# Four row tiles per VectorE operation in the FFN steps, filter products handed out by a time quota, and the columns of a small table made first

## The chip, the cores and the metric

The kernel runs on one core of a Trainium2 chip. The metric is the device time of one execution in microseconds (us). Each ratio comes with a 95% interval, and a difference counts as faster or slower only from 2% on.

Engines: PE is TensorE (PEld its weight loads), DVE is VectorE, ACT is ScalarE, POOL is GpSimd, SP issues most of the transfers. A row tile is 128 of the 2048 rows. "A step" below is one (g, m): a slice g of 256 FFN columns (18 of them) with a quarter m = 0..3 of the 16 row tiles, 72 steps in all. PSUM is the memory that the matmuls write into: each piece of work takes one of its buffers, and has to wait until the result before it has been copied out. SBUF holds all other tiles.

## The reference, cut to what matters

The function is a gated mix of two branches on one input, and the kernel computes its output and the gradients of seven inputs.

```python
g = _sigmoid((x * gate_w).sum(-1, keepdims=True))
a = irfft2(rfft2(x) * (w_r + 1j * w_i))            # filter branch, 2048 x 576
b = (gelu(x @ w_gate) * (x @ w_up)) @ w_down       # FFN branch, F = 4608
return g * a + (1 - g) * b                         # and the VJP of all this
```

In the kernel the Fourier transforms are matmuls against tables that it makes itself (cosines and sines of D columns, of 16-point columns "B", and so on). They are woven into the 72 FFN steps, so that PE always has one of three kinds of work: FFN matmuls (`xy`, `z`), weight-gradient pieces (`wps`), and Fourier matmuls (`fx`, `pf`).

## The kernel before: the parts concerned

The elementwise work of a step, once for each two row tiles: four operations before the two sigmoids, eight after them.

```python
def H_ew1(xy, q):
    xb, s, hu = (ewt(n) for n in ("xb", "s", "hu"))
    nc.scalar.copy(xb[:], xy[:, :, 0:FG]); nc.scalar.copy(hu[:], xy[:, :, FG:2 * FG])
    V.tensor_scalar(s[:], q[:], A_GELU, 1.0, ...)         # q = gate half squared, made by ACT
    V.tensor_tensor(s[:], xb[:], s[:], op=ALU.mult)
    ... # two more on q
def H_ew2(g, tp, tiles, da):
    nc.scalar.activation(om[:], s[:], ACT.Sigmoid, scale=-2.0 * C_GELU)
    nc.scalar.activation(s[:], s[:], ACT.Sigmoid, scale=2.0 * C_GELU)
    ... # eight DVE operations make A, dHg, dHu
```

The order of work in a step (cut). `sig0` and `sig1` are the two halves' sigmoids; after each of them DVE gets up to three filter products, whatever they cost. `hs` are the weight-gradient pieces of the step.

```python
def side_work():
    for _ in range(3):
        if side:
            side.pop(0)()
...
jobs = [(0, sig0)] * bool(carry) + carry + [(1.7, second)] + [(0, sig0)] * (not carry) + hs
```

The weight-gradient pieces of a slice: four down-projection pieces d, four pieces w, a small rest. Each needs one of the two PSUM buffers of the pool `pw` and gives it back when ACT (now and then DVE) has copied the piece out (`dwd`, `dw`). The last line spreads them over the four steps m = 0..3 of the next slice.

```python
pw = ps1.enter_context(tc.tile_pool(name="pw", bufs=2, space=PSUM, **kw))
...
return [[d[0]], [d[1], w[0]], [d[2], d[3], tl_], [w[1], w[2]], w[3]]
```

## Time and profile before

| | before |
|---|---|
| time, median of 4 runs beside the change | 1488.5 us (1486.2 to 1490.6) |
| span of the profiled run | 1480.0 us |
| PE busy | 1406.3 us (95%) |
| DVE busy | 880.3 us (59%) |
| ACT busy | 724.3 us (49%) |
| granted TensorE clock, mean | 0.983 |

PE bounds the kernel, so time can be won only from PE's waits and from its slow clock. The windows of the kernel before show where those lie: in 240 to 640 us, the steps that carry both filter work and weight gradients, PE is busy 373 of 400 us and the clock is 0.96; from 640 us on it is nearly full.

```profile
core 0: us, PE busy (x) PEld busy (x) DVE busy (x) ACT busy (x) POOL busy (x), PEclk, DMA share, GB/s
...
240.00:640.00 400.00, 372.84 (x2854) 256.05 (x2852) 325.59 (x879) 281.29 (x551) 36.16 (x57) 0.96 0.48 125
640.00:1030.00 390.00, 388.69 (x3274) 280.81 (x3272) 290.44 (x793) 265.25 (x527) 39.21 (x61) 1.00 0.55 142
```

### The profile page before, as it was taken

How to read it: one execution, taken by the hardware profiler on the slowest of the kernel's cores; microseconds unless marked ns; L12 is line 12 of the kernel's file. 1: busy time of each engine (PE TensorE's matmuls, PEld its weight loads, DVE VectorE, ACT ScalarE, POOL GpSimd, SP SyncE). 2: the span in 40 equal slices, each digit the busy share in tenths (PEclk: the TensorE clock that was granted, in tenths of full speed). 3: DMA queues.
4: the chain of work that ended last, by engine and by line, in shares of the span. 5: the costliest groups of instructions: out<-in, count | busy, mean ns of one | idle time of the engine just before them, and what ended most of it. 6: DMA issues, size and time to landing. Idle time of an engine off the chain costs nothing.

```text
span 1480.0 us, 29784 instructions
## 1 busy us (share of the span) xinstructions
PE 1406.3 (95%) x11412; PEld 1028.8 (70%) x11412; DVE 880.3 (59%) x2359; ACT 724.3 (49%) x1424; POOL 126.0 (9%) x230
## 2 busy tenths in 40 slices
PE   6789899898999999999999999999999999999998
PEld 4446576575675675677777777677877777777776
DVE  6598668978877878867777778775000561212110
ACT  5587568577676677667767766664000000000000
POOL 2101010010010010010010011000000110000000
PEclk9999999999999999999999999999999999999999
DMA  5154344554455454354545545656999997777773
GB/s 191 52 142 129 98 117 124 134 136 126 125 137 123 126 137 127 101 142 129 129 132 149 149 134 150 171 142 140 267 201 202 200 220 163 163 161 163 157 155 74
DMA packets 519990, 215.21 MB, mean 145 GB/s; under 512 B 316296, under 2 KB 514056, under 8 KB 519848
## 3 DMA queue, kind: packets, MB, share of 16 engines
q1 hardware_dynamic: 510216, 192.80, 55.9%
q0 software_dynamic: 7824, 19.49, 4.4%
q8 instruction: 89, 1.46, 0.4%
q10 hardware_dynamic: 1808, 1.02, 0.2%
q14 instruction: 53, 0.43, 0.1%
HBM read 40.90 MB, written 93.84 MB: 91 GB/s over the span
## 4 chain that ended last, share of the span: by engine, by line
PE 77%; DVE 14%; ACT 5%; issue 2%; DMA 1%; POOL 0%; SPq 0%; DVEq 0%; ACTq 0%; POOLq 0%
PE acc L1084 28%; PE xy L385 14%; PE wps L496 12%; PE wps L479 7%; PE z L373 6%; PE wps L509 2%; PE xy L380 2%; PE z L376 1%; DVE sn L703 1%; DVE sm L703 1%; DVE om L438 1%; DVE A L436 1%; ACT da L398 1%; DVE s L412 1%; PE fx L547 1%
## 5 line engine op out<-in xcount | busy, mean ns | idle before, releaser
L1084 PEld LDWEIGHTS <-pin 128*128 128x128 bf16 x3456 | 338.0, 98 | 86.2 <-DMA pin<-scr 1.2
L385 PE MATMUL xy<-wgu,xT 128*128 128x512 bf16 x1152 | 282.7, 391 | 0.0
L496 PEld LDWEIGHTS <-xn 128*128 128x128 bf16 x2304 | 224.7, 98 | 31.1 <-issue 0.2
L385 PEld LDWEIGHTS <-xT 128*128 128x128 bf16 x1152 | 109.2, 100 | 145.5 <-issue 43.3
L398 ACT ACTIVATE da<-z,omg 128x256 bf16<-128x256 f32 x288 | 113.3, 475 | 112.0 <-PE z L376 110.3
L1101 ACT COPY bo<-acc 128x288 f32<-128x288 f32 x32 | 12.8, 399 | 309.1 <-PE acc L1084 309.1
L479 PE MATMUL wps<-dB,A 128*128 128x288 bf16 x1152 | 155.2, 289 | 0.0
L373 PE MATMUL z<-wdT,dOT 128*128 128x256 bf16 x1152 | 139.4, 275 | 13.4 <-ACT Y L554 7.2
L1084 PE MATMUL acc<-wgT,pin 128*128 128x288 bf16 x1152 | 143.6, 286 | 0.0
L1084 PE MATMUL acc<-wuT,pin 128*128 128x288 bf16 x1152 | 143.6, 286 | 0.0
L1084 PE MATMUL acc<-wd_all,pin 128*128 128x288 bf16 x1152 | 142.8, 286 | 0.9 <-DMA pin<-scr 0.9
L479 PEld LDWEIGHTS <-A 128*128 128x128 bf16 x1152 | 113.5, 99 | 37.6 <-issue 2.5
L373 PEld LDWEIGHTS <-dOT 128*128 128x128 bf16 x1152 | 111.8, 98 | 32.1 <-issue 13.6
L496 PE MATMUL wps<-dHg,xn 128*128 128x256 bf16 x1152 | 133.0, 273 | 0.0
L496 PE MATMUL wps<-dHu,xn 128*128 128x256 bf16 x1152 | 132.0, 272 | 0.0
L404 ACT ACTIVATE q<-xy 128x512 bf16<-128x512 f32 x144 | 86.8, 603 | 63.9 <-PE xy L385 62.9
L428 ACT ACTIVATE om<-s 128x512 bf16<-128x512 bf16 x144 | 92.6, 643 | 51.7 <-DVE s L412 51.7
L1161 DVE SCALAR_TENSOR_TENSOR f32t<-gwf,dlog,b16t 128x576 f32<-128x576 f32 x16 | 13.1, 818 | 173.9 <-DMA b16t<-dxa_scr 173.9
L411 DVE TENSOR_SCALAR s<-q 128x512 bf16<-128x512 bf16 x144 | 41.9, 291 | 89.5 <-ACT q L404 89.2
L429 ACT ACTIVATE s<-s 128x512 bf16<-128x512 bf16 x144 | 90.7, 630 | 4.6
L412 DVE TENSOR_TENSOR s<-xb,s 128x512 bf16<-128x512 bf16 x144 | 61.2, 425 | 52.5 <-ACT xb L409 46.0
L502 POOL DMA_DIRECT2D out_dram<-dw x67 | 48.8, 729 | 458.9 <-ACT dw L457 334.0
(196 smaller groups left out, 1762.9 us busy)
## 6 DMA issues: line engine op xcount, KB each, us to landing
scr<-A SPq DMA_DIRECT2D x144, 128.0 KB, 2.1
scr<-dHg SPq DMA_DIRECT2D x144, 128.0 KB, 2.1
scr<-dHu SPq DMA_DIRECT2D x144, 128.0 KB, 2.2
out_dram<-dw POOLq DMA_DIRECT2D x67, 128.0 KB, 2.4
wd_all<-in_B_w_down_dram SPq DMA_DIRECT2D x3, 1728.0 KB, 14.3
out_dram<-dwd POOLq DMA_DIRECT2D x34, 144.0 KB, 2.2
scr_p<-Vt SPq DMA_DIRECT2D x32, 145.0 KB, 2.9
wgu<-in_B_w_gate_dram SPq DMA_DIRECT2D x18, 256.0 KB, 3.3
```

Of the source, the lines that this page charges most:

```text
L373: nc.tensor.matmul(zo(t), lhsT=dOT[:, ci, t, :], rhs=wdT[:, ci, :], start=(t % 4 < 2 and ci == 0), stop=False)
L385: nc.tensor.matmul(xy[k][:, t % 2, :], lhsT=xT[:, ci, t, :], rhs=wgu[:, ci, :], start=False, stop=(ci == 3))
L398: nc.scalar.activation(da[:, tt, :], z[:, tt, k, :], ACT.Copy, scale=omg32[:, t:t + 1])
L404: nc.scalar.activation(q[:], xy[:, :, 0:FG], ACT.Square)
L411: V.tensor_scalar(s[:], q[:], A_GELU, 1.0, op0=ALU.mult, op1=ALU.add)
L412: V.tensor_tensor(s[:], xb[:], s[:], op=ALU.mult)
L428: nc.scalar.activation(om[:], s[:], ACT.Sigmoid, scale=-2.0 * C_GELU)
L429: nc.scalar.activation(s[:], s[:], ACT.Sigmoid, scale=2.0 * C_GELU)
L479: nc.tensor.matmul(wps[:, :288], lhsT=tl(0, t)[:, fch * P:(fch + 1) * P], rhs=dB[:, t, h * 288:(h + 1) * 288], start=(t == 0), stop=(t == ...
L496: nc.tensor.matmul(wps[:, cc, :], lhsT=xn[:, t, (c0 + cc) * P:(c0 + cc + 1) * P], rhs=tl(k, t), start=(t == 0), stop=(t == T - 1))
L502: wst[0].dma_start(ov[:, c0:c0 + TPB, fsl], dw[:])
L1084: nc.tensor.matmul(acc[:, :288], lhsT=src[:, r, :], rhs=w_of(r)[:, h * 288:(h + 1) * 288], start=(first and r == 0), stop=(last and r == F ...
```

## The change

Its intent is to make DVE lighter and its work more even: (1) the FFN elementwise work in operations on four row tiles, with a formula of 2 + 9 operations in place of 4 + 8; (2) filter products in 14 units of known length, handed out by a quota of 1.4 us at two places a step; (3) the copies of a tail table moved from DVE to ACT; (4) the columns of table B made at the very start and the rest of B inside the loop. Larger tiles need SBUF, so fewer are kept, and the weight-gradient pieces were put in another order so that the `A` tiles come free sooner. Cut to its core:

```diff
-    keepA = ... bufs=13      # two row tiles each
+    keepA = ... bufs=6       # four row tiles each
 def H_ew1 / H_ew2:           # now on [P, 4, FG] tiles, q, s and om with one buffer
-        V.tensor_tensor(q[:], xb[:], q[:], op=ALU.mult)
 ...
+        V.tensor_tensor(xb[:], xb[:], s[:], op=ALU.mult)
+        V.tensor_tensor(q[:], xb[:], q[:], op=ALU.mult)
         V.tensor_tensor(om[:], om[:], q[:], op=ALU.mult)
-        V.tensor_scalar(om[:], om[:], 1.0, None, op0=ALU.add)
 ...
+        V.tensor_tensor(om[:], om[:], s[:], op=ALU.add)
+        V.tensor_tensor(hu[:], da[:], hu[:], op=ALU.mult)
+        V.tensor_tensor(dHg[:], hu[:], om[:], op=ALU.mult)
 # weight-gradient pieces for m = 0, 1, 2, 3
-        return [[d[0]], [d[1], w[0]], [d[2], d[3], tl_], [w[1], w[2]], w[3]]
+        return [[d[0]], [d[1], d[2], d[3]], [w[0], tl_], [w[1], w[2]], w[3]]
 # quota
-            def side_work():
-                for _ in range(3):
-                    if side:
-                        side.pop(0)()
+            def side_work(us):
+                while side and us > 0:
+                    us -= side[0][0]
+                    side.pop(0)[1]()
 # order in a step: one pair of sigmoids, after the first job behind `second`
-                jobs = [(0, sig0)] * bool(carry) + carry + [(1.7, second)] + [(0, sig0)] * (not carry) + hs
+                jobs = carry + [(1.7, second)] + hs
                 for w, f in jobs:
                     ...
                     f()
+                    if f is not second and state and late:
+                        late.pop()()
 # tail table
-        V.tensor_copy(tb.Oi[:, :, 0:P], tp_[:, :, 0:P])        # and three more
+        nc.scalar.copy(tb.Oi[:, :, 0:P], tp_[:, :, 0:P])
 # head
     build_D(nc, tb, unit, res, 0, 2)
+    columns_B(nc, tb, res)
     build_D(nc, tb, unit, res, 2, 2)
 ...
+        if t == 13:
+            build_B(nc, tb, unit, res)
-    build_B(nc, tb, unit, res)
```

More of the change, by code (lines that the diff above doesn't have):

```diff
@@ L75, in iotas @@
     nc.vector.tensor_scalar(tb.dn[:], tb.dcol[:], 1.0 / D, None, op0=ALU.mult)
-    tb.krow = res.tile([P, 32, 2, 2], F32, name="krow")
+    kk = tb.kk = unit([2, P], F32, name="kk")
+    tb.krow = kk[:, 0, :].rearrange("p (g k c) -> p g k c", k=2, c=2)
     for v in range(2):
@@ L79, in iotas @@
     G.memset(tb.krow[:, 0, 1, :], 32.0)
-    tb.kadd = res.tile([P, 64, 2], F32, name="kadd")
-    G.iota(tb.kadd[:], pattern=[[0, 64], [S // 4, 2]], base=S // 4, channel_multiplier=0, **kw)
+    tb.kadd = kk[:, 1, :].rearrange("p (k c) -> p k c", c=2)
+    G.iota(tb.kadd, pattern=[[0, 64], [S // 4, 2]], base=S // 4, channel_multiplier=0, **kw)
     tb.scol = res.tile([P, T], F32, name="scol")
@@ L145, in build_R @@
     X = unit([n, P], I32, name="XR")
-    krow, kadd = tb.krow[:].rearrange("p g k c -> p (g k c)"), tb.kadd[:].rearrange("p k c -> p (k c)")
+    krow, kadd = tb.kk[:, 0, :], tb.kk[:, 1, :]
     for t in range(n):
@@ L154, in build_R, with columns_B @@
     tb.Rt += [tb.Rpair[:, t0 % 8 + t, :] for t in range(n)]
-def build_B(nc, tb, unit, res):
+def columns_B(nc, tb, res):
     V, G = nc.vector, nc.gpsimd
-    kw = dict(allow_small_or_imprecise_dtypes=True)
     col = res.tile([P, 12], F32, name="bcol")
@@ L188, in build_B @@
     tt(m1, u_, k_, ALU.add)
+    tb.bcols = (k_, nt, a0, a1, b1, m0, m1)
+def build_B(nc, tb, unit, res):
+    V, G = nc.vector, nc.gpsimd
+    kw = dict(allow_small_or_imprecise_dtypes=True)
+    k_, nt, a0, a1, b1, m0, m1 = tb.bcols
     k2 = unit([2, 2, 16, 2], F32, name="k2B")
@@ L242 @@
     o5v = out_5[0:512, :].rearrange("(c p) f -> p c f", p=P)
-    scr = [[dram.tile([TPB, P, FF], BF16, name=f"scr{k}_{tp}") for tp in range(NT)] for k in range(3)]
+    scr = [[dram.tile([4, P, FF], BF16, name=f"scr{k}_{m}") for m in range(T // 4)] for k in range(3)]
     a_scr = dram.tile([S, D], BF16, name="a_scr")
@@ L297 @@
     load_w(0, 0)
-    gwb = res.tile([P, D], BF16, name="gwb")
     ew = wstack.enter_context(tc.tile_pool(name="ew", bufs=2))
-    keepA = wstack.enter_context(tc.tile_pool(name="keepA", bufs=13))
-    keep = wstack.enter_context(tc.tile_pool(name="keep", bufs=16))
+    keepA = wstack.enter_context(tc.tile_pool(name="keepA", bufs=6))
+    keep = wstack.enter_context(tc.tile_pool(name="keep", bufs=8))
     stage = wstack.enter_context(tc.tile_pool(name="stage", bufs=2))
@@ L389, in ewt, with H_act, H_ew1 @@
     def ewt(tag):
-        return ew.tile([P, TPB, FG], BF16, tag=tag, name=tag, bufs=3 if tag in ("da", "xb") else 2)
+        return ew.tile([P, 4, FG], BF16, tag=tag, name=tag, bufs=1 if tag in ("q", "s", "om") else 2)
     def H_da(m, z):
-        das = []
-        for k in range(2):
-            da = ewt("da")
-            for tt in range(TPB):
-                t = 4 * m + 2 * k + tt
-                nc.scalar.activation(da[:, tt, :], z[:, tt, k, :], ACT.Copy, scale=omg32[:, t:t + 1])
-            das.append(da)
-        return das
-    def H_q(xy):
-        q = ewt("q")
-        nc.scalar.activation(q[:], xy[:, :, 0:FG], ACT.Square)
-        return q
-    def H_ew1(xy, q):
-        xb, s, hu = (ewt(n) for n in ("xb", "s", "hu"))
-        nc.scalar.copy(xb[:], xy[:, :, 0:FG])
-        nc.scalar.copy(hu[:], xy[:, :, FG:2 * FG])
+        da = ewt("da")
+        for t in range(4):
+            nc.scalar.activation(da[:, t, :], z[:, t % 2, t // 2, :], ACT.Copy, scale=omg32[:, 4 * m + t:4 * m + t + 1])
+        return da
+    def H_act(k, xy, tiles, part):
+        xb, q, hu = tiles
+        h = slice(2 * k, 2 * k + 2)
+        if part == 0:
+            nc.scalar.activation(q[:, h, :], xy[:, :, 0:FG], ACT.Square)
+        else:
+            nc.scalar.copy(xb[:, h, :], xy[:, :, 0:FG])
+            nc.scalar.copy(hu[:, h, :], xy[:, :, FG:2 * FG])
+    def H_ew1(tiles):
+        xb, q, hu = tiles
+        s = ewt("s")
         V.tensor_scalar(s[:], q[:], A_GELU, 1.0, op0=ALU.mult, op1=ALU.add)
@@ L413, in H_ew1 @@
         V.tensor_scalar(q[:], q[:], 6.0 * A_GELU * C_GELU, 2.0 * C_GELU, op0=ALU.mult, op1=ALU.add)
-        V.tensor_tensor(q[:], xb[:], q[:], op=ALU.mult)
-        return xb, q, s, hu
+        return s
     stores = []
@@ L423, in flush, with H_ew2 @@
             n -= 1
-    def H_ew2(g, tp, tiles, da):
-        xb, q, s, hu = tiles
+    def H_ew2(g, m, tiles, s, da):
+        xb, q, hu = tiles
         om = ewt("om")
@@ L429, in H_ew2 @@
         nc.scalar.activation(s[:], s[:], ACT.Sigmoid, scale=2.0 * C_GELU)
-        A = keepA.tile([P, TPB, FG], BF16, tag="A", name="A")
-        dHg = keep.tile([P, TPB, FG], BF16, tag="dHg", name="dHg")
-        dHu = keep.tile([P, TPB, FG], BF16, tag="dHu", name="dHu")
+        A = keepA.tile([P, 4, FG], BF16, tag="A", name="A")
+        dHg = keep.tile([P, 4, FG], BF16, tag="dHg", name="dHg")
+        dHu = keep.tile([P, 4, FG], BF16, tag="dHu", name="dHu")
+        V.tensor_tensor(xb[:], xb[:], s[:], op=ALU.mult)
+        V.tensor_tensor(q[:], xb[:], q[:], op=ALU.mult)
         V.tensor_tensor(om[:], om[:], q[:], op=ALU.mult)
-        V.tensor_scalar(om[:], om[:], 1.0, None, op0=ALU.add)
-        V.tensor_tensor(xb[:], xb[:], s[:], op=ALU.mult)
         V.tensor_tensor(A[:], xb[:], hu[:], op=ALU.mult)
-        V.tensor_tensor(om[:], om[:], s[:], op=ALU.mult)
-        V.tensor_tensor(om[:], om[:], hu[:], op=ALU.mult)
-        V.tensor_tensor(dHg[:], da[:], om[:], op=ALU.mult)
         V.tensor_tensor(dHu[:], da[:], xb[:], op=ALU.mult)
+        V.tensor_tensor(om[:], om[:], s[:], op=ALU.add)
+        V.tensor_tensor(hu[:], da[:], hu[:], op=ALU.mult)
+        V.tensor_tensor(dHg[:], hu[:], om[:], op=ALU.mult)
         fsl = slice(g * FG, (g + 1) * FG)
@@ L443, in store @@
             for k, tl in enumerate((A, dHg, dHu)):
-                LD.dma_start(scr[k][tp][:, :, fsl].rearrange("t p f -> p t f"), tl[:])
+                LD.dma_start(scr[k][m][:, :, fsl].rearrange("t p f -> p t f"), tl[:])
         stores.append(store)
@@ L463, in tl @@
         def tl(k, t):
-            return kt[t // TPB][k][:, t % TPB, :]
+            return kt[t // 4][k][:, t % 4, :]
         dwd_tiles, wp = {}, {}
@@ L520, in W_units @@
         if g == 0:
-            return [[w[0], tl_], [w[1], d[0]], [d[1], d[2], d[3]], [w[2], w[3]], []]
-        return [[d[0]], [d[1], w[0]], [d[2], d[3], tl_], [w[1], w[2]], w[3]]
+            return [[w[0], tl_], d, [w[1]], [w[2]], w[3]]
+        return [[d[0]], [d[1], d[2], d[3]], [w[0], tl_], [w[1], w[2]], w[3]]
     side = []
@@ L585, in tail_table @@
             nc.tensor.transpose(tp_[0:n, c, 768:768 + 32], tb.Dt[3][0:32, c, P:HF], ident[0:32, 0:32])
-        V.tensor_copy(tb.Oi[:, :, 0:P], tp_[:, :, 0:P])
-        V.tensor_copy(tb.Oi[:, :, P:HF], tp_[:, :, 512:512 + n])
+        nc.scalar.copy(tb.Oi[:, :, 0:P], tp_[:, :, 0:P])
+        nc.scalar.copy(tb.Oi[:, :, P:HF], tp_[:, :, 512:512 + n])
         ot = unit([2, HF], name="ot")
-        V.tensor_copy(ot[0:n, :, 0:P], tp_[0:n, :, 256:256 + P])
-        V.tensor_copy(ot[0:n, :, P:HF], tp_[0:n, :, 768:768 + n])
+        nc.scalar.copy(ot[0:n, :, 0:P], tp_[0:n, :, 256:256 + P])
+        nc.scalar.copy(ot[0:n, :, P:HF], tp_[0:n, :, 768:768 + n])
         for c in range(2):
@@ L693, in comb, with stack @@
                 return f
-            def stack(k1, k2, conj):
+            def stack(k1, k2, conj, j):
                 def f():
-                    m1, m2 = st[p, k1], st.pop((p, k2))
-                    o = unit([2, 2, DF], name="s" + k1)
-                    for j in range(2):
-                        J = slice(64 * j, 64 * j + 64)
-                        for c, op in enumerate(signs(conj)):
-                            V.tensor_tensor(o[64 * c:64 * c + 64, :, j, :], m1[J, :, c, :], m2[J, :, 1 - c, :], op=op)
-                    st[p, k1] = o
+                    m1, m2 = st[p, k1], st[p, k2]
+                    if j == 0:
+                        st[p, "s" + k1] = unit([2, 2, DF], name="s" + k1)
+                    o = st[p, "s" + k1]
+                    J = slice(64 * j, 64 * j + 64)
+                    for c, op in enumerate(signs(conj)):
+                        V.tensor_tensor(o[64 * c:64 * c + 64, :, j, :], m1[J, :, c, :], m2[J, :, 1 - c, :], op=op)
                 return f
@@ L709, in f @@
                 def f():
-                    m = st[p, key][:].rearrange("p t j l -> p (t j) l")
+                    if key == "m1":
+                        halve(st[p, "sm1"])
+                    m = st[p, "s" + key][:].rearrange("p t j l -> p (t j) l")
                     q = unit([4, 2, HF], name="q" + key)
@@ L726, in products @@
             return [
-                lambda: halve(G),
-                mul("m1", X, W[:, 0]), mul("m2", X, W[:, 1]), stack("m1", "m2", False),
-                lambda: (halve(st[p, "m1"]), fold("m1")()),
-                mul("n1", G, W[:, 0]), mul("n2", G, W[:, 1]), lambda: (stack("n1", "n2", True)(), fold("n1")()),
-                mul("o1", G, X[:, :, 0, :]), mul("o2", G, X[:, :, 1, :]), comb("o1", "o2", True),
-                out_dw,
+                (0.9, lambda: (halve(G), mul("m1", X, W[:, 0])())), (0.8, mul("m2", X, W[:, 1])),
+                (0.85, stack("m1", "m2", False, 0)), (0.85, stack("m1", "m2", False, 1)), (1.2, fold("m1")),
+                (0.8, mul("n1", G, W[:, 0])), (0.8, mul("n2", G, W[:, 1])),
+                (0.85, stack("n1", "n2", True, 0)), (0.85, stack("n1", "n2", True, 1)), (1.1, fold("n1")),
+                (0.8, mul("o1", G, X[:, :, 0, :])), (0.8, mul("o2", G, X[:, :, 1, :])), (0.85, comb("o1", "o2", True)),
+                (0.0, out_dw),
             ]
@@ L863 @@
             x2[t - 2]()
+    run_late(tb)
     x2[T - 2]()
-    build_B(nc, tb, unit, res)
-    run_late(tb)
     x2[T - 1]()
@@ L936 @@
             hs = [h for u in pend[m] for h in u] if pend else []
-            def side_work():
-                for _ in range(3):
-                    if side:
-                        side.pop(0)()
+            def side_work(us):
+                while side and us > 0:
+                    us -= side[0][0]
+                    side.pop(0)[1]()
             if g == 0 and m > 0:
@@ L944 @@
             z, xy_full = H_mm(g, m)
+            tiles = [ewt(tag) for tag in ("xb", "q", "hu")]
             xy = xy_full(0)
-            das = H_da(m, z)
-            q = H_q(xy)
+            da = H_da(m, z)
+            H_act(0, xy, tiles, 0)
             flush()
@@ L953 @@
                 fft_next()
-            ta = H_ew1(xy, q)
+            H_act(0, xy, tiles, 1)
             state = []
-            def sig0():
-                H_ew2(g, 2 * m, ta, das[0])
-                side_work()
-                state.append(None)
             def second():
@@ L965, in second, with sigs @@
                     fft_next()
-                state.insert(0, H_ew1(xy, H_q(xy)))
-            def sig1():
-                H_ew2(g, 2 * m + 1, state[0], das[1])
-                side_work()
+                for part in range(2):
+                    H_act(1, xy, tiles, part)
+                state.append(H_ew1(tiles))
+                side_work(1.4)
+            def sigs():
+                H_ew2(g, m, tiles, state[0], da)
+                side_work(1.4)
             if g == 0:
@@ L973 @@
                 fft_next()
-                sig0()
-                sig1()
+                sigs()
             else:
-                jobs = [(0, sig0)] * bool(carry) + carry + [(1.7, second)] + [(0, sig0)] * (not carry) + hs
+                jobs = carry + [(1.7, second)] + hs
                 us = sum(j[0] for j in jobs)
-                at, k, late = 0.0, 1, [sig1]
+                at, k, late = 0.0, 1, [sigs]
                 for w, f in jobs:
@@ L983 @@
                         k += 1
-                        if len(state) == 2 and late:
-                            late.pop()()
                     f()
                     at += w
+                    if f is not second and state and late:
+                        late.pop()()
                 while k <= n:
@@ L990 @@
                     k += 1
-                if late:
-                    sig1()
+                assert not late
             carry = []
@@ L996 @@
                 load_w(g + 1, m)
-            if pr == 3:
-                LD.dma_start(gwb[:], gate_w.partition_broadcast(P))
             if (g, m) in ((0, 3), (1, 0)):
@@ L1020, in pin @@
         tl = p2in.tile([P, FCB, P], BF16, tag="pin", name="pin")
-        LD.dma_start_transpose(tl[:], scr[k][t // TPB][t % TPB][:, f0 * P:(f0 + FCB) * P])
+        LD.dma_start_transpose(tl[:], scr[k][t // 4][t % 4][:, f0 * P:(f0 + FCB) * P])
         return tl
@@ L1068 @@
         gwf = p2res.tile([P, D], F32, name="gwf")
-        V.tensor_copy(gwf[:], gwb[:])
         wT_loads = [(k, r0) for k in range(NB) for r0 in (0, 6)]
@@ L1076, in b16t, with load_gwf @@
             return p2b.tile([P, D], BF16, tag="b16t", name="b16t")
+        def load_gwf():
+            gwb = b16t()
+            LD.dma_start(gwb[:], gate_w.partition_broadcast(P))
+            V.tensor_copy(gwf[:], gwb[:])
         def acc_pair():
@@ L1190 @@
                 load_wuT(*wT_loads.pop(0))
+            if i == 8:
+                load_gwf()
             lead = lead and kind != "u"
```

## The prediction

> **What bounds the kernel now.** I read the page first: over the span of 1480.0 us TensorE (PE) is busy 1406.3 us (95%), VectorE (DVE) 59%, ScalarE (ACT) 49%. So a faster DVE is worth nothing by itself; only PE's idle 73.7 us, and whatever makes its matmuls slow, can be won. The slices show where: DVE and ACT work only up to about 1040 us; the last 30% (matmuls of line 1084) is PE at 100% and the change leaves it alone. Next the table of who waited for whom on PE over the whole span (engine line waited for: total us, times, longest):
>
> ```profile
> PE pf L744 <- ACT da L398: 25.4, 7, 4.7
> PE xy L380 <- ACT g_bf L354: 7.8, 1, 7.8
> PE z L373 <- ACT Y L554: 7.2, 4, 2.1
> ...
> PE z L373 <- DVE ot L590: 4.3, 1, 4.3
> PE pf L564 <- ACT ve L568: 1.9, 1, 1.9
> PE z L373 <- ACT Vt L747: 1.7, 1, 1.7
> ```
>
> Seven stalls, one for each of seven filter passes, make 25.4 us. The timeline around the first one tells what they are:
>
> ```profile
> 284.37 0.43 DVE L412 TENSOR_TENSOR s<-xb,s 128x512 bf16<-128x512 bf16 x1
> ...
> 284.83 0.63 ACT L428 ACTIVATE om<-s 128x512 bf16<-128x512 bf16 x1 [4.77 <-DVE s L412]
> ...
> 286.03 1.55 ACT L398 ACTIVATE da<-z,omg 128x256 bf16<-128x256 f32 x4
> ...
> 287.63 0.64 PE L744 MATMUL pf<-qn,BTtab 128*128 128x290 bf16 x2 [4.75 <-ACT da L398]
> ...
> 288.07 3.62 PE L385 MATMUL xy<-wgu,xT 128*128 128x512 bf16 x8
> ...
> 300.75 1.90 PE L385 MATMUL xy<-wgu,xT 128*128 128x512 bf16 x8
> ```
>
> Read backwards: the filter matmul needs the PSUM buffer that z and the FFT share; `da` empties it, but stands on ACT behind a sigmoid that waited 4.77 us for `s` of a late DVE. On DVE's timeline there is no gap from 254.6 to 288 us: products are issued three at a time after each of the two elementwise parts of a step, some 6 us of them in one step, on top of 9.35 us of FFN work, while a step is 13.9 us of PE. On average DVE is only 81% busy from 240 to 640 us; it is overloaded in bursts.
>
> The last two lines show a second cost: right after a stall eight matmuls took 3.62 us, elsewhere 1.90. In the chain of work the eight after the seven stalls take 3.41, 3.37, 2.96, 3.41, 3.01, 3.19 and 2.86 us against 1.83: 9.4 us more; the down-projection matmuls behind them lose 2.3 more. So the seven stalls cost 25.4 + 11.7 us.
>
> The 7.8 us is the head's end. The small table B is built there last:
>
> ```profile
> 48.75 0.17 DVE L166 CAST bcol<-bbit 128x4 f32<-128x4 int32 x1
> 49.09 0.35 POOL L170 TENSOR_SCALAR bcol<-bcol 128x1 f32<-128x1 f32 x2 [40.23 <-DVE bcol L166]
> ...
> 56.01 0.51 ACT L213 ACTIVATE oB<-XBi,pi 128x256 f32<-128x256 int32 x1 [9.57 <-DVE XBi L206]
> ...
> 58.35 0.61 PE L380 MATMUL xy<-wgu,xT 64*128 64x512 bf16 x2 [7.77 <-ACT g_bf L354]
> ```
>
> The gate's sigmoid stands on ACT behind B's sine, and PE behind the gate's PSUM buffer.
>
> **What the Trainium skill says.** "TensorE: Matmul & The Clock Gate", What's actually happening: after an idle window of about 3.4 us the array runs at half rate, until a busy window has passed. The trace agrees: the 4.75 us stall is followed by matmuls at half rate, and the granted clock of 280 to 320 us is 0.91. The same page, Architectural detail, has ACT and DVE as strict FIFOs; the trace agrees, since `da` ran only after both sigmoids. "VectorE: DVE Perf Modes", The perf-mode tier table: bf16 from SBUF, a tensor_tensor does two elements a cycle, a tensor_scalar four. The trace agrees: 425 ns at 512 elements and 757 ns at 1156 give 0.516 ns an element and some 160 ns fixed, which doubling the tile saves. "ScalarE: Activation LUTs", What ACT_TABLE_LOAD costs: an ACTIVATE is 186 ns + 0.833 ns an element; that makes 613 ns at 512, the trace has 643 and 630.
>
> **The change part by part.**
>
> 1. FFN elementwise. Groups of VectorE before (72 steps, 144 instructions a line):
>
> ```profile
> L412 DVE TENSOR_TENSOR s<-xb,s 128x512 bf16<-128x512 bf16 x144 | 61.2, 425 | 52.5 <-ACT xb L409 46.0
> L411 DVE TENSOR_SCALAR s<-q 128x512 bf16<-128x512 bf16 x144 | 41.9, 291 | 89.5 <-ACT q L404 89.2
> L682 DVE TENSOR_TENSOR o<-Xg,Xx 128x1156 bf16<-128x1156 bf16 x16 | 12.1, 757 | 0.0
> ```
>
> A step now has 18 tensor_tensor and 6 tensor_scalar: the twelve rows sum to 673 us, 9.35 us a step. After: 9 tensor_tensor of 1024 elements, estimated 425 + 512 x 0.516 = 689 ns, and 2 tensor_scalar, estimated 291 + 133 = 424 ns (512 more at four a cycle of 0.96 GHz, that page's clock): 7.05 us. Saved 2.3 us a step, 166 us of DVE in all, nearly all beside PE. The sigmoids go from four of 0.636 to two of about 1.06 us: 0.43 us of ACT a step.
>
> 2. Products by quota. A pass has 6 multiplications of 0.757, 8 stackings of 0.457, 4 folds of 0.462, a combination of 0.92 and small ones of 0.7: 11.7 us. Now each of two places a step issues units until 1.4 us are spent, in fact 1.6 to 1.7. That is 3.3 us a step, so 10.4 us of DVE against 12.5 to 13 of PE (13.9 less the stall's share). In the built program of the change qn is made in the step before the one that uses it, about 10 us ahead. For the sigmoid: the first ACT copies of the second half end about 1.2 us after its matmuls, `s` is done 1.1 later, both sigmoids 2.1 after that, `da` 2.0 later with a copy between: 6.4 us, where PE has 16 down-projection matmuls, z and xy of the next step, 6.5 us, before it wants the buffer in the tightest step. So the stalls should shrink to a few tenths. Gain: 25.4 + 11.7, with the 1.7 us of `Vt`, 38.8; I leave 1.8 for such remains: **37 us**.
>
> 3. tail_table's copies go from DVE (behind two elementwise parts) to ACT ahead of the sigmoids, four copies of about 1.1 us in sum, beside 16 matmuls of 1.96 us. The 4.3 us go, and z after it at half rate (3.60 against 1.91 us, with its small followers 2.2 in all): **6.5 us**. FFT units lie a little differently in that step, which should remove most of the 1.9 us for `ve`: **1.5 us**.
>
> 4. The head. The 7.8 us and 1.6 of slow matmuls after it should go. But the columns are now ahead of the D tables on POOL: nine tiny DVE operations take 1.3 us there, 14 POOL ones 3.5 us (49.1 to 52.6 above), and POOL makes y of tables 2 to 4 only then. Before, the cosine work on DVE ended at 6.7 us and PE's first full run of L547 began at 11.0. After: bits to 8.0, columns to 11.7, y to 13.1, DVE's X and its copies of xT to 15.9, the last table to 17.7. PE starts 6.6 us later. The rest of B in the loop costs 2 to 3 us of DVE and ACT on a path where both alternate with PE. Net 9.4 - 6.6 - 2.5 = **0.3 us**.
>
> 5. The first group (58 to 105 us) has ACT without gaps at 10.3 us a step and PE waiting 1.7 us for `Y`; 0.4 us less of ACT in three steps: **1 us**. The gate weights loaded late, the stores of four tiles and the reordered W units move nothing on PE; both programs have equal counts of PE instructions (22826 rows).
>
> Sum: 37 + 6.5 + 1.5 + 0.3 + 1 = 46 us; 1489.8 - 46 = 1444, and I add 2 for waits that single buffers of q, s and om may bring: **1446 us**.
>
> **The rivals.** (a) The stalls come back as another wait: one H_ew1 for four tiles waits for the second half, so the sigmoids come later and `da` with them. For: ACT is a FIFO and the tightest step has only 0.1 us to spare. Against: DVE has 2 us a step free, so it isn't behind when the copies arrive. Should each pass keep two stalls of 1.5 us (too short for the slow clock), 8 passes keep 24 us: about 1468. (b) The head loses: a start 6.6 us later and a longer B wait, say 5 us in all beyond my net: 1451. (c) The slow clock goes more fully than counted: granted clock 0.983 over 1480 us means 25 us lost, of which I claim 15.5; with g = 0 also free of waits: 1434. (d) Single buffers delay ACT: Square of the next step waits for DVE's third product of this one; in the tightest step both fall at about 6.5 us after the second half's matmuls, so a few tenths, and the buffer of xy is wanted again only half a step later: I expect nothing on PE.
>
> **Range and chances.** The mechanism of part 2 is shown directly and DVE gets lighter by 25%, so faster by over 2% (under 1460) has 0.86; rival (a) in earnest gives within 2%, 0.13; slower 0.01. Range 1433 to 1462.
>
> **What would show it right or wrong.** Right: line `pf <- ACT da` gone or under 3 us; DVE's FFN operations near 690 and 425 ns and its busy time down by some 165 us; granted clock at or above 0.99 between 240 and 640 us; `ot` gone from PE's waits; the first long run of PE's first table matmuls at 17 us instead of 11; `g_bf` gone. Wrong: new PE waits for `da`, `Vt` or `Xx` in every step (rival a); first FFN matmuls later than 62 us (rival b); or PE's idle time gone and the span unchanged, if matmuls run slower for another reason.

## The result, and the profile after

The changed kernel took 1497.8 us (median of 4, 1495.2 to 1500.7) against 1488.5 us before: ratio 1.0063, interval 1.0037 to 1.009. That is "same" by the 2% rule, and in fact a little slower. A ratio here is the mean of one kernel's runs over the mean of the other's runs in the same rounds, so it is not quite the ratio of the medians. Executions over 1.5% slower than the fastest of the same kernel are left out of the means. The prediction had been 1446 us.

DVE did get lighter. The groups of the kernel after (line engine operation, tiles, shapes, count; busy us, mean ns; idle before) show the new durations:

```profile
L417 DVE TENSOR_SCALAR s<-q 128x1024 bf16<-128x1024 bf16 x72 | 30.6, 426 | 188.1 <-ACT q L409 187.9
L433 ACT ACTIVATE om<-s 128x1024 bf16<-128x1024 bf16 x72 | 76.5, 1062 | 35.2 <-DVE s L418 35.1
L438 DVE TENSOR_TENSOR xb<-xb,s 128x1024 bf16<-128x1024 bf16 x72 | 49.8, 692 | 86.0 <-ACT s L434 85.5
```

692, 426 and 1062 ns, where 689, 424 and about 1060 were predicted. The eleven rows of FFN work sum to 506.6 us, 7.04 us a step. DVE's busy time is 743.5 us, 137 less than before. (The rows fell by 166 us; the busy time fell by less, because the records of operations that follow each other overlap a little: summed one by one, DVE's records fell by 170 us.)

The table of who waited for whom on PE, kernel after:

```profile
PE wps L484 <- ACT dwd L462: 21.7, 13, 2.6
PE z L380 <- ACT Y L559: 8.0, 5, 2.1
...
PE fx L552 <- ACT Dt L129: 7.2, 1, 7.2
...
PE pf L662 <- DMA Vp<-scr_x: 4.2, 1, 4.2
PE z L380 <- ACT Xg L667: 4.2, 7, 0.6
...
PE pf L662 <- ACT Vt L754: 2.6, 1, 2.6
```

The seven waits for `da` (25.4 us), `g_bf` (7.8) and `ot` (4.3) are gone, as predicted. In their place PE waits 13 times for `dwd`, a copy out of a down-projection piece, 21.7 us in all. The timeline around one of these waits, kernel after (start, duration, engine, operation; in brackets the wait and what ended it):

```profile
505.12 2.12 PE L484 MATMUL wps<-dB,A 128*128 128x288 bf16 x16
...
505.45 0.65 ACT L409 ACTIVATE q<-xy 128x512 bf16<-128x512 f32 x1
...
505.94 0.64 ACT L411 CAST xb<-xy 128x512 bf16<-128x512 f32 x1
...
507.10 0.93 DVE L709 TENSOR_TENSOR sn<-n,n 64x578 bf16<-64x578 bf16 x2
...
507.33 2.12 PE L484 MATMUL wps<-dB,A 128*128 128x288 bf16 x16
508.06 0.43 DVE L417 TENSOR_SCALAR s<-q 128x1024 bf16<-128x1024 bf16 x1
508.59 0.69 DVE L418 TENSOR_TENSOR s<-xb,s 128x1024 bf16<-128x1024 bf16 x1
...
509.31 1.06 ACT L433 ACTIVATE om<-s 128x1024 bf16<-128x1024 bf16 x1 [2.25 <-DVE s L418]
...
510.40 1.06 ACT L434 ACTIVATE s<-s 128x1024 bf16<-128x1024 bf16 x1
...
511.37 0.38 ACT L462 CAST dwd<-wps 128x288 bf16<-128x288 f32 x1
...
511.80 3.77 PE L484 MATMUL wps<-dB,A 128*128 128x288 bf16 x16 [2.35 <-ACT dwd L462]
```

Read it from the end. Three pieces d1, d2, d3 stand in this step (m = 1), and there are two PSUM buffers. d3 may start when d1 has been copied out. PE had finished d1 by about 507.2, but ACT copies it only at 511.37, since the copy was issued behind the two sigmoids of the step. These waited 2.25 us for `s`. For four row tiles `s` cannot start before the second half's `q` (done at 506.10) and `xb` (506.58), and DVE, still busy with eight operations on the step before and two units of products, came to it only at 508.06, 2.0 us after `q`. This is so before each of the six longest waits for `dwd` (1.96 to 1.97 us, then waits of 2.35 to 2.60); before the wait at 350.56 us, with the same two sigmoids ahead of the copy, DVE came at once (0.03 us after `q`), and the wait is 1.43 us. So two things make the stall: the sigmoids' place ahead of the copy, and a DVE that is late by one burst. One wait on a busy ACT and DVE was traded for another of the same kind, in the same stretch. And the stall slowed the clock: the sixteen matmuls behind it took 3.77 us against 2.12.

The windows of the kernel after (columns as in those of before) say that the stretch gained little:

```profile
240.00:640.00 400.00, 373.59 (x2905) 263.27 (x2940) 272.30 (x507) 278.38 (x500) 37.93 (x60) 0.97 0.47 127
```

PE busy is 373.6 where it was 372.8, and the clock 0.97 where it was 0.96. In this trace 87 matmul records are missing, which leaves holes of about 4 us in PE's busy time here. The weight loads, none of which is missing, give a better measure of the work done in these 400 us: 2940 against 2852, 3% more. The lengths of steps below are not touched by missing records.

For the rest of the document I use lengths of stages, read from the timeline as the starts of each step's first `z` matmuls. One trace each, us. The seven waits for `da` before, and those for `dwd` now, lie in the steps m = 1 of g = 4 to 10: six in stage C, the last in D.

| stage | before | change | quota alone | quota, head, tail | same + 2 + 9 formula | change, sigmoids later |
|---|---|---|---|---|---|---|
| A: start to second step | 68.3 | 67.4 | 69.3 | 62.4 | 62.4 | 64.7 |
| B: to start of g = 4 | 196.2 | 200.1 | 197.0 | 189.6 | 195.6 | 198.8 |
| C: g = 4 to 9 | 337.4 | 329.1 | 303.2 | 304.0 | 306.7 | 317.5 |
| D: g = 10 to last step | 405.5 | 418.7 | 400.6 | 400.6 | 401.1 | 407.6 |
| E: last step, output stage | 472.6 | 479.8 | 477.5 | 473.6 | 477.7 | 478.7 |

Stage A differs by some 3 us between traces of kernels with the same head (old head 66.1 to 69.3, the change's 64.7 to 69.2, columns after the tables 59.4 to 62.4), so differences of that size in it mean nothing.

Stage C won 8 us where some 37 were expected, and D, where nothing was expected, lost 13. In C the steps m = 1 last 16.4 us on average (17.9 before, 12.5 with the quota alone).

### The profile page after: what moved, and what is told of

Its sections match the earlier page's. It is cut to its first block, busy times and chain, and to the rows that moved or that the text cites.

```text
span 1495.0 us, 28096 instructions
## 1 busy us (share of the span) xinstructions
PE 1394.6 (93%) x11325; PEld 1029.7 (69%) x11412; DVE 743.5 (50%) x1419; ACT 709.2 (47%) x1284; POOL 124.9 (8%) x230
## 4 chain that ended last, share of the span: by engine, by line
PE 70%; ACT 12%; DVE 8%; issue 4%; DMA 3%; SPq 2%; POOL 0%; another core or an unknown queue 0%; ACTq 0%; DVEq 0%; POOLq 0%
PE acc L1092 28%; PE wps L501 12%; PE xy L392 11%; PE z L380 7%; PE wps L484 5%; ACT om L433 3%; PE xy L387 2%; ACT q L409 2%; PE wps L514 1%; DVE s L418 1%; PE z L383 1%; ACT hu L412 1%; ACT xb L411 1%; DMA pin<-scr 1%; ACT s L434 1%
## 5 line engine op out<-in xcount | busy, mean ns | idle before, releaser
L392 PE MATMUL xy<-wgu,xT 128*128 128x512 bf16 x1065 | 254.5, 379 | 9.5 <-issue 7.9
L484 PE MATMUL wps<-dB,A 128*128 128x288 bf16 x1152 | 161.6, 297 | 22.1 <-ACT dwd L462 21.7
L417 DVE TENSOR_SCALAR s<-q 128x1024 bf16<-128x1024 bf16 x72 | 30.6, 426 | 188.1 <-ACT q L409 187.9
L409 ACT ACTIVATE q<-xy 128x512 bf16<-128x512 f32 x144 | 87.1, 605 | 64.7 <-PE xy L392 59.1
L433 ACT ACTIVATE om<-s 128x1024 bf16<-128x1024 bf16 x72 | 76.5, 1062 | 35.2 <-DVE s L418 35.1
L438 DVE TENSOR_TENSOR xb<-xb,s 128x1024 bf16<-128x1024 bf16 x72 | 49.8, 692 | 86.0 <-ACT s L434 85.5
L412 ACT CAST hu<-xy 128x512 bf16<-128x512 f32 x144 | 88.5, 615 | 0.0
```

Of the source, the lines that this page charges most:

```text
L392: nc.tensor.matmul(xy[k][:, t % 2, :], lhsT=xT[:, ci, t, :], rhs=wgu[:, ci, :], start=False, stop=(ci == 3))
L409: nc.scalar.activation(q[:, h, :], xy[:, :, 0:FG], ACT.Square)
L412: nc.scalar.copy(hu[:, h, :], xy[:, :, FG:2 * FG])
L417: V.tensor_scalar(s[:], q[:], A_GELU, 1.0, op0=ALU.mult, op1=ALU.add)
L438: V.tensor_tensor(xb[:], xb[:], s[:], op=ALU.mult)
L484: nc.tensor.matmul(wps[:, :288], lhsT=tl(0, t)[:, fch * P:(fch + 1) * P], rhs=dB[:, t, h * 288:(h + 1) * 288], start=(t == 0), stop=(t == ...
```

## The experiments

Eleven kernels ran, in three groups on three chips. All outputs are right. Beside them the kernel before took 1486.6, 1482.0 and 1486.0 us; ratios are to these.

Theory A: the change loses in the `dwd` waits, because the four-tile sigmoids stand ahead of a copy that PE needs. Theory B: DVE delivers `s` too late whatever stands around the sigmoids, so if this stall is taken away another takes its place. Theory C: the new order of pieces alone does it. A further suspect is the head, where PE starts later.

**1. Sigmoids later in the changed kernel.** They, and the elementwise operations and products that follow them, are issued only when 1.7 us of weight-gradient work (so d1 and its copy) stands between them and the second half.

```diff
-                    if f is not second and state and late:
-                        late.pop()()
+                    if f is not second and state:
+                        since += w
+                        if late and since >= 1.7:
+                            late.pop()()
```

> The changed kernel, with the sigmoids (and the second elementwise part) issued once 1.7 us of weight-gradient jobs have followed the second half, instead of after the first such job; in the steps m = 0 and 1 this puts the evacuation of the first down-projection piece ahead of the sigmoids on ACT. Theory A (the new stalls are PE waiting for a PSUM buffer of the weight gradients, whose evacuation stands behind sigmoids in ACT's FIFO): the wait of the down-projection matmuls for dwd, 21.7 us in 13, falls below 5 us, the slow clock after it goes (about 10 us), 1497.8 becomes 1460 to 1475. Theory B (VectorE delivers s too late for the sigmoids whatever stands around them, so any evacuation that follows waits): the waits move to da, Xx or Vt, and the time stays within 6 us of 1498.

Measured: 1471.0 us, ratio 0.9891 (0.9876 to 0.9907), 1.7% under the change. The waits for `dwd` left the table; what stands at the head of PE's waits in this kernel now is

```profile
PE z L380 <- ACT Xx L667: 8.4, 6, 1.7
```

Theory A holds: moving the sigmoids by one piece of work is worth about 26 us (0.0172 of 1487). The 21.7 us of waits went, 8.4 us came back as waits for `Xx`, and the clock recovered (0.991 from 0.986): in 110 to 640 us it was half for 13.5 us where it was half for 27.3, an estimated 7 us of PE. In the traces stages C and D are 11.6 and 11.1 us shorter; the 2.7 in A are of the size that varies by itself. Theory B is wrong as a whole but right in part: `Xx`, a copy of the filter branch, now stands behind the same sigmoids, and before each of its five long waits (1.65 us) `s` started 1.96 to 1.97 us after its `q`, just as in the change.

**2. Columns of B after the D tables, in the changed kernel.**

```diff
     build_D(nc, tb, unit, res, 0, 2)
-    columns_B(nc, tb, res)
 ...
     build_D(nc, tb, unit, res, 4, 1)
+    columns_B(nc, tb, res)
```

> The changed kernel, with the columns of the small table computed after the last D table instead of after the first. By the head's account (PE's first table matmuls wait 7.2 us for a table whose POOL work stands behind the columns) the first z of the first group starts 5 to 6.6 us earlier than 56.6 us and the time falls by about 6 us, to 1492. If the head's later loop absorbs it (PE bound there by something else), less than 2 us.

Measured: 1490.6 us, ratio 1.0026 (1.0009 to 1.0042). The first step began at 51.6 us instead of 56.6, the second at 62.4 instead of 67.4, and the wait for `Dt` fell from 7.2 to 1.1 us. In the changed kernel's timeline that wait is plain: POOL's chain for the columns (first and last operation shown) runs to 11.2 us, and only then does POOL start the work for the next D table.

```profile
7.72 0.35 POOL L170 TENSOR_SCALAR bcol<-bcol 128x1 f32<-128x1 f32 x2 [3.89 <-DVE bcol L166]
...
11.03 0.19 POOL L173 TENSOR_TENSOR bcol<-bcol 128x1 f32<-128x1 f32 x1
11.20 0.77 POOL L122 TENSOR_SCALAR yD<-lrow,dn 128x145 f32<-128x145 f32 x2
```

So "columns first" costs about 5.5 us (0.0037 of 1487; 5.0 in the traces), and what the head gains must come from the rest of B in the loop, which no run has alone.

**3. The quota alone, on the kernel before.** Two row tiles, old formula, old head; only the 14 units and `side_work(1.4)`.

```diff
-                for _ in range(3):
-                    if side:
-                        side.pop(0)()
+                while side and us > 0:
+                    us -= side[0][0]
+                    side.pop(0)[1]()
```

> The kernel before, with nothing but the filter products in 14 units, issued by a quota of 1.4 us after each elementwise part. If the seven stalls of before come from products issued in bursts, the 25.4 us wait of the filter matmul for da falls to under 8 us, and the time from 1488.5 to 1455 to 1468, without any wider elementwise work. If they come from VectorE's total load (12.7 us of 12.6 a step), they stay above 15 us and the time within 10 us of 1488.

Measured: 1448.6 us, ratio 0.9738 (0.9721 to 0.9756), faster by 38.9 us. The `da` waits are gone, no `dwd` waits appear, and PE's waits in this kernel begin with what the kernel before had besides:

```profile
PE xy L380 <- ACT g_bf L354: 7.7, 1, 7.7
PE z L373 <- ACT Y L554: 7.2, 4, 2.1
```

Its windows, for the stretch that had the stalls:

```profile
240.00:640.00 400.00, 397.28 (x3174) 280.05 (x3173) 350.99 (x954) 309.90 (x604) 40.35 (x63) 1.00 0.53 140
```

PE is busy 397 of 400 us at clock 1.00, while DVE is at 351 of 400 us, busier than ever. The load of DVE was not what cost; its bursts were. The 37 us of the prediction are there, without any lighter DVE.

**4. Two down-projection pieces a step, in the changed kernel.**

```diff
-        return [[d[0]], [d[1], d[2], d[3]], [w[0], tl_], [w[1], w[2]], w[3]]
+        return [[d[0], d[1]], [d[2], d[3]], [w[0], tl_], [w[1], w[2]], w[3]]
```

> The changed kernel, with the four down-projection pieces two and two in the steps m = 0 and 1 (instead of one and three), the sigmoids where the change has them. Theory A: with two PSUM buffers no piece needs a buffer whose evacuation stands behind the sigmoids of its own step, so the dwd wait of 21.7 us falls below 6 us and the time to 1462 to 1480. Theory B: waits elsewhere, time within 6 us of 1498.

Measured: 1475.8 us, ratio 0.9926 (0.9911 to 0.9941). The waits for `dwd` fell to 1.3 us, those of `z` for `Xx` rose to 9.2. A second, independent way of taking those waits away gives nearly as much, which supports A.

**5. Quota, head and tail table together, two row tiles, old formula.** The kernel of run 3 with the tail copies on ACT, the columns of B after the last D table and the rest of B in the loop.

```diff
-        V.tensor_copy(tb.Oi[:, :, 0:P], tp_[:, :, 0:P])
+        nc.scalar.copy(tb.Oi[:, :, 0:P], tp_[:, :, 0:P])
 ...
     build_D(nc, tb, unit, res, 4, 1)
+    columns_B(nc, tb, res)
 ...
+        if t == 13:
+            build_B(nc, tb, unit, res)
```

> The kernel before with three parts of the change and without the rest: the products by quota, the four copies of the tail table on ACT, and the small table made in the head's loop, its columns after the last D table. Expected from the runs so far: e3's 1448.6, less 6.9 us for the head (first group's second z at 62.4 us in e2 against 69.3 in e3), less 3.6 for the tail table (that step is 13.85 us in the changed kernel, 17.4 before): 1438. If the parts get in one another's way (the stall returns as another wait), 1444 or more.

Measured: 1430.1 us, ratio 0.9647 (0.9631 to 0.9663). This is the fastest kernel and beats both. Against run 3 stage A is 6.9 us shorter (some 3 of it can be chance, see above), and the step with the tail table takes 12.95 us instead of 17.43. The three largest real waits of PE in this kernel lie in the head and in the first slice (before 110 us), where the change and the kernel before have them as well:

```profile
PE z L380 <- ACT Y L561: 7.2, 4, 2.1
PE tp L342 <- DMA xn<-in_A_x_dram: 4.9, 1, 4.9
PE tp L345 <- DVE Vt L578: 4.2, 2, 2.3
```

**6. The quota with the change's order of pieces, two row tiles.** Theory C's test. (The first slice's order changed too, as in the change.)

```diff
-        return [[d[0]], [d[1], w[0]], [d[2], d[3], tl_], [w[1], w[2]], w[3]]
+        return [[d[0]], [d[1], d[2], d[3]], [w[0], tl_], [w[1], w[2]], w[3]]
```

> The quota kernel (e3), elementwise by two row tiles as before, but with the order of the weight-gradient pieces that the change needs for its smaller pool (one, three, then the others). Theory A (only the evacuation of the first piece behind BOTH sigmoids of four tiles makes the wait): with two tiles the first evacuation stands behind one pair of sigmoids whose input is long ready, 3.4 us after the second half's matmuls, before PE wants the buffer at 3.9 us; so at most 5 us over e3's 1448.6. Theory C (the order of the pieces alone costs it, three pieces on two buffers): 15 us or more over e3, with waits for dwd of 10 us or more.

Measured: 1440.0 us, ratio 0.9717 (0.9703 to 0.9732). In PE's waits of this kernel those for `dwd` are 4.2 us, five in number:

```profile
PE wps L479 <- ACT dwd L457: 4.2, 5, 1.5
```

Three pieces in one step cost no time over run 3 where the sigmoids are for two row tiles. Theory C falls: the 21.7 us take the order and the four-tile work together.

**7. The quota with the 2 + 9 formula, two row tiles.**

```diff
-        V.tensor_tensor(q[:], xb[:], q[:], op=ALU.mult)     # before the sigmoids
-        V.tensor_scalar(om[:], om[:], 1.0, None, op0=ALU.add)
+        V.tensor_tensor(q[:], xb[:], q[:], op=ALU.mult)     # after them
+        V.tensor_tensor(om[:], om[:], s[:], op=ALU.add)     # and the rest of the change's H_ew2
```

> The quota kernel (e3) with the change's new formula, 2 + 9 VectorE operations, but still on two row tiles (one operation of 0.29 us fewer per pair). VectorE is not the bound once the bursts are gone, so within 3 us of e3's 1448.6, with VectorE's busy time down by some 42 us. If it still were the bound, 5 us or more off.

Measured: 1449.1 us, ratio 0.9775 (0.976 to 0.9789), against 0.9738 for run 3 on another chip; the intervals just miss each other. DVE is busy 829 us instead of 879. Fifty microseconds less of DVE bring no gain.

**8. Run 5 with the 2 + 9 formula.**

> e5 and e7 together, everything of the change but the four row tiles and what their pools need. Expected 1438, as e5, within 3 us; the candidate for a kernel better than both.

Measured: 1440.7 us, ratio 0.9724 (0.9701 to 0.9748), on the same chip and in the same rounds as run 5's 0.9647. So the formula costs some 11 us here; run 7 against run 3, on two chips, gave 5.5 (0.0037 of 1482). The stages put 6.0 of it in B and 2.7 in C (the 4.1 in E I don't trust, see below). PE's waits in this kernel hold two that run 5's do not:

```profile
PE pf L663 <- ACT Vt L755: 2.9, 1, 2.9
...
PE pf L570 <- ACT Y L560: 1.9, 1, 1.9
```

Which part of the formula does it, the operation moved behind the sigmoids or the later `dHg`, I did not test.

**9. Both mends in the changed kernel** (runs 1 and 2 together).

> The changed kernel with both mends together: sigmoids emitted later (measured alone: ratio 0.9891 against 1.0063 for the change) and the B columns after the D tables (alone: 1.0026). Theory A (two separate costs that add): 1.0063 - 0.0172 - 0.0037 = 0.9854. Rival (the two hide each other, or the start of the loop is limited by something else): 0.989 or more. Either way above the 0.9647 of quota, head and tail at two row tiles, if the four-tile FFN work itself is what costs.

Measured: 1464.6 us, ratio 0.9855 (0.9834 to 0.9877), where 0.9854 was expected from the sum: within the interval the two costs are separate. The kernel is still 31 us (0.0208 of 1486) above run 5. In PE's waits of this kernel the largest that run 5 lacks is

```profile
PE z L380 <- ACT Xx L667: 9.5, 6, 1.7
```

These are six waits in stage C, one at the end of each step m = 1.

**10. Sigmoids in halves again, in the changed kernel.** `s` and its sigmoids for two row tiles at a time, the first half as early as before, everything else on four.

```diff
-        nc.scalar.activation(om[:], s[:], ACT.Sigmoid, scale=-2.0 * C_GELU)
-        nc.scalar.activation(s[:], s[:], ACT.Sigmoid, scale=2.0 * C_GELU)
+        nc.scalar.activation(om[:, h], s[:, h], ACT.Sigmoid, scale=-2.0 * C_GELU)   # h: two row tiles
+        nc.scalar.activation(s[:, h], s[:, h], ACT.Sigmoid, scale=2.0 * C_GELU)
```

> The changed kernel with s and its two sigmoids in halves of two row tiles again (first half as soon as its copies are there), the rest of the elementwise work still over four. Theory A (the wait is the length of ACT work for the four tiles, ahead of the evacuation of a weight-gradient piece): 1.3 us of sigmoids instead of 2.1 stand there and they start on earlier data, so the dwd waits of 21.7 us fall to some 10 and the ratio from 1.0063 to about 0.998. Rival (only the place of the evacuation after any sigmoid counts, not the length): dwd waits stay near 20 us, ratio 1.006; ACT has 0.43 us a step more to do, which could make it 1.008.

Measured: 1480.2 us, ratio 0.9958 (0.9943 to 0.9973). The waits shrank less than I expected, the time more. From PE's waits in this kernel:

```profile
PE wps L489 <- ACT dwd L467: 16.1, 13, 2.7
```

And from its windows:

```profile
240.00:640.00 400.00, 378.28 (x3016) 269.35 (x3052) 289.19 (x608) 298.52 (x579) 38.99 (x62) 1.00 0.49 134
```

The timeline and the clock give the reason: six of the seven waits in the steps m = 1 of g = 4 to 10 are 1.3 to 1.8 us here, and matmuls behind all seven run at full rate (clock 1.00). In the changed kernel six of seven are 2.35 us or longer, and behind five of those six the matmuls run at half rate, in whole or in part. So the cost of this stall is the wait plus a slow clock.

Whether the second part is paid can be read from the record of the granted clock. In each trace its changes lie whole multiples of 3.41 us apart. In all thirteen traces, from 110 us to the end of the matmuls, a piece of 3.41 us at full clock in which PE was idle for 1.98 us or more was always followed by half clock, and one with less than 1.95 us of idle time never. So a stall counts by what of it falls into one such piece. The wait of 2.35 us that cost nothing more (403.75 us) falls into two, 1.43 and 0.92 us; the wait of 2.69 us in run 10 splits into 1.21 and 1.48; waits of 1.3 to 1.8 us are too short wherever they fall.

**11. Run 5 with the change's order of pieces.**

> The kernel before with quota, the tail table on ACT, the B columns after the last D table, and the change's order of weight-gradient pieces. The order alone measured 0.9717 against 0.9738 for the quota alone, so if parts add: 0.9647 - 0.0021 = 0.9626. If the gain of e6 was the luck of one chip: 0.965 to 0.967.

Measured: 1437.1 us, ratio 0.9672 (0.9651 to 0.9693), beside 0.9647 for run 5 on another chip. No gain: run 6's 0.9717 against 0.9738 was not a gain of the order.

## Why the prediction was wrong, point by point

**Part 1, durations and load of DVE: right.** 7.05 us a step predicted, 7.04 measured; 166 us predicted, 166.5 measured in the rows. (The sign "busy time down by some 165 us" forgot that the records overlap: 137.) What was wrong was to take this as free. Four tiles and the new formula together cost time on PE: about 26 us through the place of the sigmoids (run 1), and the 31 us that remain between runs 9 and 5. Of these the formula may be 5 to 11 (runs 7 and 8, if it costs the same at four tiles). The rest goes with waits for other copies and loads in stages B to D, of which `Xx` is the largest; that is read from the tables, not tested.

**Part 2, the quota: the mechanism and its size are right, its survival was not.** The failed step is "So the stalls should shrink to a few tenths", with the one behind it, "I leave 1.8 for such remains". Alone the quota brings 38.9 us (run 3) against 37 predicted. In the change stage C gains 8, and PE waits 21.7 us for `dwd`. The check of ACT's queue before that step followed the sigmoid only to `da` and the buffer of `z`. It took `s` as done 1.1 us after the second half's first copies, where the timeline above has 2.7 us after `xb`. It did not follow the sigmoid to the other copies in the same queue, and it was done for one step with 16 down-projection matmuls, while the reordered pieces put 48 into step m = 1 with two PSUM buffers. Part 5 said that the reordered units "move nothing on PE"; at two row tiles that is nearly true (waits for `dwd` of 4.2 and 2.7 us in runs 6 and 11, no time), at four it is false.

**Part 3, the tail table: right.** 6.5 us predicted; stage B is 7.4 us shorter in run 5 than in run 3, 4.5 of it in the step with the table (3.6 in the change). Most of the 1.5 us for `ve` came in the change: PE waits 0.8 us for it in all, where it waited 2.2 (run 5 still has 2.2).

**Part 4, the head: right in both halves, as far as traces that differ by 3 us can tell.** PE's first long run of table matmuls began at 17.17 us instead of 11.00 (6.6 us later predicted, 6.2 measured), the first step 8.5 us later, the second 0.9 earlier: net as good as nothing, as predicted. What I did not see is that the two halves can be had apart (run 5).

**Part 5, the first group: right, but not the end of it.** The three steps after its first are 0.8 us shorter together (1 predicted), and the step behind them is 3.2 us longer; one wait for `Y` there grew from 1.5 to 3.6 us.

**Rival (a) is what happened, at another buffer,** at 22 us of waits where it had 24. I gave it 0.13, for three reasons. It was argued against with "DVE has 2 us a step free, so it isn't behind when the copies arrive": in the timeline above DVE is 2.0 us behind, because a mean of free time says nothing about a burst of eight 0.69 us operations in a row. Its stalls were taken as 1.5 us, "too short for the slow clock"; six were 2.35 us or more, and five of them were followed by it. And it looked for the wait at `da` alone. Even so its 1468 us was 30 us too low: it had no cost for the formula and for waits outside the filter passes (stage D lost 13 us; run 1 gives 11 of them back). **Rival (b)** was wrong (the first step began at 56.6 us), **(c)** did not come (mean clock 0.986 against 0.983), **(d)** is not seen as a line of its own. Two small readings were off: DVE does not stop at 1040 us (in the kernel before it is busy 85.6 of the 400 us from 1030 on), and there are eight filter passes, of which seven had the stall.

**Open.** Stage E, where the change moves little but the load of the gate weights and the layout of the stored tiles, is 472.5 to 480.7 us in all the traces; waits for `pin` loads vary between none and 5.6 us. Some of that may be chance from run to run (472.5 to 477.7 with the old output stage alone); I have one trace of each kernel. One-time losses in stage B (a load of `Vp` that PE waited 4.2 us for, 1.0 before; in the trace its transfer was issued behind stores that waited for a late `dHg`) I have read, not tested. Why the 2 + 9 formula costs time is not settled. And no run takes four row tiles with the old formula, or with two buffers of q, s and om, so what four tiles cost by themselves once the sigmoids stand later is not shown.

## What to carry to other kernels

Where an engine off the critical path only holds up the bound engine in bursts, spread its work before making it lighter: the quota alone brought 2.6% with DVE as loaded as ever, and 50 us less of DVE on top of it (run 7) brought nothing. An operation on twice the data can't start before the later half is there and holds an in-order queue for longer (a sigmoid here 1062 ns for 643), so before coarsening one, list everything that is issued behind it in the same queue and which buffer each of those gives back. And test the parts of a bundled change one by one, since here three good parts (3.5% together in run 5, one of them at a better place) were hidden by the rest.

## What the Trainium skill lacked or had wrong

- "TensorE: Matmul & The Clock Gate", What's actually happening, gives a free-running window of about 3.4 us and the half rate after at least one idle window. The window is seen here (the changes of the clock lie whole multiples of 3.41 us apart), but it need not be all idle: about 1.96 us of idle time in one was the border in thirteen traces (run 10 above). In the changed kernel six of the seven waits of 2.35 to 2.64 us for `dwd` and `Vt` were followed by matmuls at half rate (the worst 3.77 us for sixteen, against 2.12). In run 10 waits of 1.3 to 1.8 us for `dwd` were followed by full rate each time, and so was one of 2.69 us that fell half into each of two windows. So a stall of over 2 us is to be priced with the slow clock, though not every one pays it.
- "ScalarE: Activation LUTs", What ACT_TABLE_LOAD costs, and "VectorE: DVE Perf Modes", The perf-mode tier table: nothing wrong. An ACTIVATE of 1024 elements took 1062 ns where the first page's sum, 186 ns + 0.833 ns an element, gives 1039; tensor_tensor and tensor_scalar took 692 and 426 ns.
- What a larger tile costs in an in-order queue has no number on any page. "Perfetto Trace Analysis", Optimizing Scalar/DVE Operations, does give the advice: where ACT or DVE are not saturated but cause bubbles on other engines, breaking up instructions may let work finish sooner. The runs agree: here two sigmoids of 1.06 us and their wait of 2.25 us for `s` held back a 0.38 us copy; moving them behind it was worth 1.7%, breaking them up (run 10) 1.0%.
